# Pinning the whole instruction order of an attention and feed-forward kernel by a flat list, with one buffer pool and fewer loads

## The chip, the cores and the metric

The kernel runs on one core of a Trainium2 chip. The metric is the device time of one execution in microseconds (us), less being better; a profile of one execution goes with it.

## The reference

A recurrent attention over 4 x 8 heads of size 48 and 768 steps is followed, per token, by a two-layer feed-forward network with an unusual activation:

```python
for t in range(S):
    state = alpha[:, :, t, :, None] * state + np.einsum('bhd,bhe->bhde', k[:, :, t], v[:, :, t])
    y[:, :, t] = np.einsum('bhd,bhde->bhe', q[:, :, t], state)
...
h = x @ w_in                       # x: 3072 x 384 (y by token), w_in: 384 x 2048
sp = np.maximum(h, 0.0) + np.log1p(np.exp(-np.abs(h)))
g = h * erf(sp)
return (g @ w_out).astype(np.float32)
```

The inputs q, k, v and alpha are float32; w_in and w_out are float64 and arrive as pairs of 32-bit integers.

## The kernel before, in words

**The attention** is computed in 24 chunks of 64 steps for 2 of the 4 batch entries at once (two runs of 12 chunks). In `Chunk`, `ld` (L151) loads alpha, k and q with two loads each, one per half of the partitions, into one set of raw buffers. `a1` (L159) scans alpha into its running product A on VectorE, and GpSimd copies A's last column to `ae` (L165). `a2` (L170 to L176) makes the reciprocal of A: Relu for a check, Ln and Exp on ScalarE, then a correction in two VectorE operations. `a3` (L180 to L186) loads v and multiplies k and q into K and Q. `a4` multiplies K by Q (`pS`, L202) and the previous chunk's K by v (`pu`, L211) on TensorE, brings the state T forward on VectorE (L221 to L227), masks `pS` into `sT` (L229) and transposes K (`pn`, L235; `kn`, L239). `a5` (L260) makes y on TensorE from T, Q, sT and v, and `put` (L284, L285) splits it into `x_hi` (ScalarE) and `x_lo` (VectorE).

**The feed-forward network** runs over 12 blocks of 256 tokens, two chunks each, in `Moe`. Every product is made in three matmuls of rounded high and low parts. For each of 4 groups g of 512 hidden columns: `H` (L320), two halves of 18 matmuls, each copied out by ScalarE (`hs`, L325); `U` (Tanh, L331); `L1` (two Ln and an Exp, L336 to L338); `L2` (VectorE, L344, L345); `G` (Gelu, L348); `Z` (VectorE, L352, L353); `O` (two halves: `gh` by a copy, L366 or L368, `gl` by a subtraction, L369, and 12 matmuls into `acc`, L377). `out` (L385, L386) copies the two accumulators and stores them. Tanh and Gelu need one ScalarE table, Ln and Exp another; `new_phase` (L117) loads a table (L120) and `tab` keeps the table's functions on its own side of it.

**The weights** come in 12 pieces of w_in (512 columns) and 16 of w_out (384 columns): a load (L400), then ScalarE and VectorE turn the float64 bits into float32 (L406 to L414) and into a high and a low part (L389, L390).

**The order** is written as three lists of whole steps, START, ORDER (run for blocks 2 to 10) and TAIL (L27 to L48), which `run` (L513) issues one after the other; the framework's scheduler then sets the instructions' order on each engine from priorities that follow it, and may let a later one pass. The buffers are split by purpose: raw, K, Q, A and `ae` for the attention; pools of 4 KB buffers (per partition) of their own for s (5), hs (7), w (4) and t (1) (L70 to L77), which weights being converted share. All loads and stores are issued by SP's queue.

Of the kernel before, what the change touches and what calls it, by code (L numbers as in the profile page):

```python
# [20 lines left out]
AHI = 1e15  # L21
# [5 lines left out]
START, ORDER, TAIL = (  # L27
    z.split()
    for z in (
# [15 lines left out]
    )  # L45
)
# [3 lines left out]
def gla_moe(ctx: ExitStack, tc: tile.TileContext, q, k, v, alpha, w_in, w_out, out):  # L50
# [3 lines left out]
    M, CPB, _, D, NP, NI, TC = q.shape  # L54
    P = NI * TC
# [9 lines left out]
    NG = NF // GT  # L65
    HD = 64
# [15 lines left out]

    ra = raw.tile([P, NP * NI, 1 + TC], F32, name="raw_a")
    rq, rk = (raw.tile([P, NP, NI, TC], F32, name=f"raw_{nm}") for nm in "qk")
    for t, fill in ((ra, 1.0), (ra[:, :, 0], 0.0), (rq, 0.0), (rk, 0.0)):
        nc.vector.memset(t, fill)
# [10 lines left out]
    fixed = const.tile([P, 3], F32, name="fixed")  # L97
    bhi, bhalf, ones = (fixed[:, n : n + 1] for n in range(3))
    for t, val in ((bhi, -AHI), (bhalf, 0.5), (ones, 1.0)):
        nc.gpsimd.memset(t, val)  # L100
# [14 lines left out]
    phase = {"cur": [], "prev": []}  # L115

    def new_phase(table):  # L117
        phase["prev"] = phase["cur"]
        phase["cur"] = []
        tab(nc.scalar.preload_act_table_set(table))  # L120
        phase["prev"] = phase["cur"]
        phase["cur"] = []

    def tab(ins):
        for p in phase["prev"]:
            tc.add_manual_dep(ins.ins, p.ins.name, NOSYNC, reason="tables")
        phase["cur"].append(ins)
        return ins

    T = at.tile([P, NI * NP * HD], F32, name="T", tag="T", bufs=1)
# [6 lines left out]
    class Chunk:  # L139
# [6 lines left out]
        def ld(self):  # L146
            self.ra, self.rq, self.rk = ra, rq, rk
            for t, src in ((self.ra[:, :, 1:], alpha), (self.rk, k), (self.rq, q)):
                t = t if src is alpha else t.rearrange("p a i t -> p (a i) t")
                for par in range(2):  # L150
                    nc.sync.dma_start(  # L151
                        out=t[par * HD : par * HD + D],
                        in_=src[self.m, self.c, par].rearrange("d a i t -> d (a i) t"),
                    )

        def a1(self):
            self.A = at.tile([P, NP * NI, 1 + TC], F32, name="A", tag="A")
            flat = "p s t -> p (s t)"
            nc.vector.tensor_tensor_scan(  # L159
                out=self.A.rearrange(flat), data0=self.ra.rearrange(flat), data1=lower.rearrange(flat), initial=1.0,  # L160
                op0=ALU.mult, op1=ALU.max,
            )

            self.ae = at.tile([P, NI, NP], F32, name="ae", tag="ae")
            nc.gpsimd.tensor_copy(out=self.ae, in_=self.A[:, :, TC].rearrange("p (a i) -> p i a", a=NP))  # L165

        def a2(self):
            A = self.A[:, :, 1:]
            r = at.tile([P, NP * NI, TC], F32, name="r", tag="r", bufs=1)
            nc.scalar.activation(r, A, AF.Relu, bias=-AHI, accum_out=flags[:, self.n, 1:2])  # L170
            tab(nc.scalar.activation(r, A, AF.Ln))  # L171
            tab(nc.scalar.activation(r, r, AF.Exp, scale=-1.0, accum_out=flags[:, self.n, 0:1]))
            self.K = at.tile([P, NP, NI, TC], F32, name="K", tag="K")
            w = self.K.rearrange("p a i t -> p (a i) t")
            nc.vector.tensor_tensor(out=w, in0=A, in1=r, op=ALU.mult)
            nc.vector.scalar_tensor_tensor(out=w, in0=w, scalar=2.0, in1=r, op0=ALU.subtract, op1=ALU.mult)  # L176

        def a3(self):
            self.vv = raw.tile([P, NI * NP * HD + H * D], F32, name="raw_v", tag="raw_v", bufs=2)
            nc.sync.dma_start(out=self.vv, in_=v[self.m, self.c])  # L180
            flat = "p a i t -> p (a i t)"
            w = self.K.rearrange(flat)
            nc.vector.tensor_tensor(out=w, in0=self.rk.rearrange(flat), in1=w, op=ALU.mult)  # L183
            self.Q = at.tile([P, NP, NI, TC], F32, name="Q", tag="Q")
            flat = "p a i t -> p (a i) t"
            nc.vector.tensor_tensor(  # L186
                out=self.Q.rearrange(flat), in0=self.rq.rearrange(flat), in1=self.A[:, :, 1:], op=ALU.mult
            )

        def a4(self):  # L190
            K, Q = self.K, self.Q
# [6 lines left out]
            for pair in range(NP):  # L198
# [7 lines left out]
                if before:  # L206
                    vt = before.vv[:, NI * NP * HD :]
                    for half in range(2):
                        for i in range(NI):
                            toks, h = slice(i * TC, (i + 1) * TC), 2 * pair + (half ^ i)  # L210
                            nc.tensor.matmul(  # L211
                                out=pu[i][half * HD : (half + 1) * HD, pair * D : (pair + 1) * D],
                                lhsT=before.kn[toks, pair, half, :], rhs=vt[toks, h * D : (h + 1) * D],
                                start=True, stop=True,
                            )
            if before:
                aeb = before.ae.unsqueeze(3).broadcast_to([P, NI, NP, D])
# [395 lines left out]
```

## Time and profile before

| | us |
|---|---|
| median of 3 runs | 580.14 (580.12 to 580.36) |
| the profiled execution | 580.21 |
| its span, first to last instruction | 578.5 |
| TensorE (PE) matmuls busy | 515.2 |
| VectorE (DVE) busy | 482.5 |
| ScalarE (ACT) busy | 463.5 |
| GpSimd (POOL) busy | 51.1 |
| granted TensorE clock, mean | 0.972 of full |

Busy time is the time in which an engine has at least one instruction under way; neighbours overlap a little. The profile also tells what each engine waited for, follows the chain of waits back from the last instruction, and groups instructions by line.

### The profile page before, as it was taken

How to read it: one execution, taken by the hardware profiler on the slowest of the kernel's cores; microseconds unless marked ns; L12 is line 12 of the kernel's file. 1: busy time of each engine (PE TensorE's matmuls, PEld its weight loads, DVE VectorE, ACT ScalarE, POOL GpSimd, SP SyncE). 2: the span in 40 equal slices, each digit the busy share in tenths (PEclk: the TensorE clock that was granted, in tenths of full speed). 3: DMA queues.
4: the chain of work that ended last, by engine and by line, in shares of the span. 5: the costliest groups of instructions: out<-in, count | busy, mean ns of one | idle time of the engine just before them, and what ended most of it. 6: DMA issues, size and time to landing. Idle time of an engine off the chain costs nothing.

```text
span 578.5 us, 16974 instructions
## 1 busy us (share of the span) xinstructions
PE 515.2 (89%) x7386; PEld 496.8 (86%) x7386; DVE 482.5 (83%) x688; ACT 463.5 (80%) x706; POOL 51.1 (9%) x40
## 2 busy tenths in 40 slices
PE   0569769289999999999999999999999999999875
PEld 0458669289999999999999999999999999999775
DVE  6889879999989959969979789789699689477890
ACT  4458796689979789789699599599698797898951
POOL 2000000000000401300000400400302200000000
PEclk9999988779999999999999999999999999999988
DMA  6757434523213213211222122123022010000000
GB/s 195 229 195 222 130 114 126 157 66 83 80 30 98 65 26 92 93 43 43 75 60 74 44 61 76 42 60 103 16 62 88 1 48 30 1 1 28 28 0 33
DMA packets 36370, 43.64 MB, mean 75 GB/s; under 512 B 21952, under 2 KB 25024, under 8 KB 36288
## 3 DMA queue, kind: packets, MB, share of 16 engines
q1 hardware_dynamic: 36288, 42.48, 25.0%
q8 instruction: 60, 0.98, 0.7%
q14 instruction: 22, 0.18, 0.1%
HBM read 37.75 MB, written 4.72 MB: 73 GB/s over the span
## 4 chain that ended last, share of the span: by engine, by line
PE 61%; ACT 16%; DVE 16%; issue 5%; DMA 2%; DVEq 0%; ACTq 0%; SPq 0%
PE ph L320 27%; PE acc L377 22%; PE py L260 4%; PE pS L202 3%; ACT s L331 2%; ACT L120 2%; ACT s L336 2%; PE pu L211 2%; DVE w L345 2%; PE pn L235 2%; ACT hs L325 2%; ACT w L338 1%; ACT r L171 1%; DVE wbuf L411 1%; DVE t L344 1%
## 5 line engine op out<-in xcount | busy, mean ns | idle before, releaser
L320 PE MATMUL ph<-x_hi,wi_hi 128*128 128x256 f32 x576 | 166.9, 291 | 7.6 <-ACT x_hi L284 5.5
L320 PE MATMUL ph<-x_lo,wi_hi 128*128 128x256 f32 x576 | 164.8, 286 | 1.0 <-DVE x_lo L285 1.0
L320 PE MATMUL ph<-x_hi,wi_lo 128*128 128x256 f32 x576 | 164.6, 286 | 0.0
L377 PE MATMUL acc<-wo_hi,gh 128*128 128x384 f32 x384 | 132.5, 345 | 13.0 <-DVE gh L366 8.6
L377 PE MATMUL acc<-wo_hi,gl 128*128 128x384 f32 x384 | 130.1, 342 | 2.6 <-DVE gl L369 2.6
L377 PE MATMUL acc<-wo_lo,gh 128*128 128x384 f32 x384 | 130.6, 340 | 0.0
L320 PEld LDWEIGHTS ph<-x_hi,wi_hi 128*128 128x128 f32 x576 | 111.8, 194 | 10.2 <-ACT x_hi L284 5.9
L320 PEld LDWEIGHTS ph<-x_lo,wi_hi 128*128 128x128 f32 x576 | 112.0, 194 | 1.4 <-DVE x_lo L285 1.3
L320 PEld LDWEIGHTS ph<-x_hi,wi_lo 128*128 128x128 f32 x576 | 111.8, 194 | 0.4 <-DVE wi_lo L390 0.2
L325 ACT ACTIVATE hs<-ph 128x512 f32<-128x512 f32 x96 | 56.7, 591 | 45.6 <-PE ph L320 44.2
L377 PEld LDWEIGHTS acc<-wo_hi,gh 128*128 128x128 f32 x384 | 73.9, 192 | 14.1 <-DVE gh L366 8.8
L165 POOL COPY ae<-A 128x8 f32<-128x8 f32 x24 | 48.7, 2028 | 417.4 <-DVE T L227 338.7
L369 DVE TENSOR_TENSOR gl<-hs,gh 128x512 fp32r<-128x512 f32 x96 | 64.3, 686 | 19.2 <-ACT gh L368 16.5
L377 PEld LDWEIGHTS acc<-wo_hi,gl 128*128 128x128 f32 x384 | 73.0, 192 | 4.7 <-DVE gl L369 4.6
L377 PEld LDWEIGHTS acc<-wo_lo,gh 128*128 128x128 f32 x384 | 73.9, 192 | 0.1
L344 DVE TENSOR_TENSOR t<-s,w 128x1024 f32<-128x1024 f32 x48 | 58.6, 1220 | 12.4 <-ACT w L338 12.2
L202 PE MATMUL pS<-Q,K 48*64 48x64 f32 x768 | 39.1, 235 | 26.0 <-DVE K L183 25.5
L368 ACT ACTIVATE gh<-hs 128x512 fp32r<-128x512 f32 x72 | 45.3, 629 | 18.5 <-PE acc L377 14.4
L202 PEld LDWEIGHTS pS<-Q,K 48*64 48x64 f32 x768 | 33.0, 145 | 30.9 <-DVE K L183 21.8
L345 DVE SCALAR_TENSOR_TENSOR w<-t,w 128x1024 f32<-128x1024 f32 x48 | 58.5, 1218 | 0.4
L352 DVE TENSOR_TENSOR s<-s,w 128x1024 f32<-128x1024 f32 x48 | 58.2, 1217 | 0.0
L353 DVE SCALAR_TENSOR_TENSOR hs<-s,hs 128x1024 f32<-128x1024 f32 x48 | 58.1, 1216 | 0.1
(63 smaller groups left out, 831.9 us busy)
## 6 DMA issues: line engine op xcount, KB each, us to landing
raw_v<-in_v_dram SPq DMA_DIRECT2D x24, 448.0 KB, 3.9
wst<-in_moe_w_in_dram SPq DMA_DIRECT2D x12, 512.0 KB, 4.7
wst<-in_moe_w_out_dram SPq DMA_DIRECT2D x16, 384.0 KB, 3.8
raw_a<-in_alpha_dram SPq DMA_DIRECT2D x48, 96.0 KB, 3.0
raw_k<-in_k_dram SPq DMA_DIRECT2D x48, 96.0 KB, 2.6
raw_q<-in_q_dram SPq DMA_DIRECT2D x48, 96.0 KB, 2.2
out_dram<-o SPq DMA_DIRECT2D x24, 192.0 KB, 2.0
```

The source lines that it names most:

```text
L165: nc.gpsimd.tensor_copy(out=self.ae, in_=self.A[:, :, TC].rearrange("p (a i) -> p i a", a=NP))
L202: nc.tensor.matmul(out=ps[half * HD : (half + 1) * HD, pair * NI + i, :], lhsT=K[rows, pair, i, :], rhs=Q[rows, pair, i, :], start=True, s ...
L260: nc.tensor.matmul(out=py[i][c0 : c0 + 32, kt, :], lhsT=left[r0 : r0 + rows, at0 : at0 + 32], rhs=right[r0 : r0 + rows, pair, i, :], start ...
L320: nc.tensor.matmul(out=o, lhsT=wt[:, kt, fs], rhs=xt[:, kt, :], start=n == 0, stop=n == 3 * KT - 1)
L325: nc.scalar.activation(self.hs[g][:, sl], ph, AF.Copy)
L344: nc.vector.tensor_tensor(out=t, in0=s, in1=w, op=ALU.mult)
L345: nc.vector.scalar_tensor_tensor(out=w, in0=t, scalar=2.0, in1=w, op0=ALU.add, op1=ALU.mult)
L352: nc.vector.tensor_tensor(out=s, in0=s, in1=w, op=ALU.mult)
L353: nc.vector.scalar_tensor_tensor(out=h, in0=s, scalar=RT2 / 2, in1=h, op0=ALU.subtract, op1=ALU.mult)
L368: nc.scalar.activation(ghf, gg, AF.Copy)
L369: nc.vector.tensor_tensor(out=gl.rearrange("p a t -> p (a t)"), in0=gg, in1=ghf.bitcast(F32), op=ALU.subtract)
L377: nc.tensor.matmul(out=self.acc[tt][:, :DM], lhsT=gt[:, u, ts], rhs=wt[:, f, :], start=f == 0 and n == 0, stop=f == NF - 1 and n == 2,)
```

## The change

1. The three lists become one flat list, SCHED, of 1846 parts. Each step is now a generator that yields after every part on one engine (a group of 6 or 9 matmuls, one ScalarE or VectorE operation, a load), and naming a step in the list issues its next part. The scheduler is told to keep that order on every engine. The order itself is a different one, no longer the same from block to block.
2. ScalarE's table is loaded wherever the next function in the list needs the other one (`act`), instead of in named phases.
3. One pool `big` of 19 buffers of 4 KB serves s, hs, w, t, the loaded weights, their work buffers, and k with q.
4. alpha comes as one load of all 128 partitions, with its first column and its unused rows filled in on the host, into one of three buffers; k and q come together as one load. The scan runs in place, k and q are multiplied in place, the reciprocal has a buffer `rw` of its own, and T's product reads A's last column itself, without GpSimd's copy. The memsets of the raw buffers are gone.
5. Several buffers become single (`at`, L71, has one buffer for each tag now).

```diff
-START, ORDER, TAIL = (
...
+SCHED = """
+la_0 a1_0 a2_0 la_1 a2_0 a2_0 la_2 a1_1 a1_2 lq_0 a3_0 a2_0 wi_9 wi_9 wi_9 a2_0 wi_9 wi_5 wi_5 wi_5 a2_1 a2_1 a2_0
+a4_0 wi_11 wi_11 wi_9 wi_11 wi_9 wi_5 wi_11 wi_8 wi_8 a2_1 wi_8 wi_0 wi_0 lv_0 wi_0 wi_5 a4_0 a5_0 a4_0 wi_0 a2_1 wi_4
...
+lq_6 lv_6 a1_7 O_0_1_0 O_0_1_0 O_0_1_1 O_0_1_1 G_0_2 U_1_0 L2_0_3 L1_1_0 wo_9 wo_9 a2_6 H_1_2_0 H_2_2_0 H_2_2_0 wo_14
...
+O_11_2_0 Z_11_3 O_11_2_1 O_11_2_1 O_11_2_1 O_11_2_1 Z_11_3 O_11_3_0 O_11_3_0 O_11_3_1 O_11_3_1 O_11_3_0 O_11_3_0
+O_11_3_1 O_11_3_1 out_11_0 out_11_0 out_11_1 out_11_1
+"""
...
+    NBIG, NA = 19, 3
...
-    raw = fast.enter_context(tc.tile_pool(name="raw", bufs=1))
-    at = fast.enter_context(tc.tile_pool(name="at", bufs=2))
+    raw = fast.enter_context(tc.tile_pool(name="raw", bufs=2))
+    at = fast.enter_context(tc.tile_pool(name="at", bufs=1))
...
-    keep_s = fast.enter_context(tc.tile_pool(name="keep_s", bufs=NG + 1))
-    keep_h = fast.enter_context(tc.tile_pool(name="keep_h", bufs=2 * NG - 1))
-    keep_w = fast.enter_context(tc.tile_pool(name="keep_w", bufs=NG))
-    tmp = fast.enter_context(tc.tile_pool(name="tmp", bufs=1))
+    big = fast.enter_context(tc.tile_pool(name="big", bufs=NBIG))
...
-    for t, fill in ((ra, 1.0), (ra[:, :, 0], 0.0), (rq, 0.0), (rk, 0.0)):
-        nc.vector.memset(t, fill)
...
+    loaded = [None]
+
+    def act(table, *args, **kw):
+        if loaded[0] != table:
+            loaded[0] = table
+            nc.scalar.preload_act_table_set(table)
+        nc.scalar.activation(*args, **kw)
...
-        def ld(self):
...
+        def la(self):
+            self.A = raw.tile([P, NP * NI, 1 + TC], F32, name="A", tag="A", bufs=NA)
+            nc.sync.dma_start(out=self.A.rearrange("p s t -> p (s t)"), in_=alpha[self.m, self.c].rearrange("p a i t -> p (a i t)"))
+            yield
+
+        def lq(self):
+            self.kq = big.tile([P, 2, NP, NI, TC], F32, name="kq", tag="big")
+            nc.sync.dma_start(
+                out=self.kq.rearrange("p w a i t -> p (w a i t)"),
+                in_=qk[self.m, self.c].rearrange("p w a i t -> p (w a i t)"),
+            )
+            yield
...
         def a1(self):
...
-            self.ae = at.tile([P, NI, NP], F32, name="ae", tag="ae")
-            nc.gpsimd.tensor_copy(out=self.ae, in_=self.A[:, :, TC].rearrange("p (a i) -> p i a", a=NP))
+            a, floor = (z.rearrange("p s t -> p (s t)") for z in (self.A, lower))
+            nc.vector.tensor_tensor_scan(out=a, data0=a, data1=floor, initial=1.0, op0=ALU.mult, op1=ALU.max)
+            yield
...
+            kk = self.kq[:, 0].rearrange("p a i t -> p (a i) t")
+            nc.vector.tensor_tensor(out=kk, in0=kk, in1=w, op=ALU.mult)
+            yield
...
-                aeb = before.ae.unsqueeze(3).broadcast_to([P, NI, NP, D])
+                ae = before.A[:, :, TC].rearrange("p (a i) -> p i a", a=NP)
+                aeb = ae.unsqueeze(3).broadcast_to([P, NI, NP, D])
...
         def L1(self, g):
             s = self.s[g]
...
+            act(LNEXP, s, s, AF.Ln, scale=0.5 - 2.0**-24, bias=0.5)
+            yield
+            self.w[g] = w = self.pl.w.tile([P, GT * TB], F32, name="w", tag=self.pl.tag("w"))
+            act(LNEXP, w, s, AF.Ln, scale=-1.0)
+            yield
+            act(LNEXP, w, w, AF.Exp, scale=-1.0)
+            yield
...
-    run(START, 0, 0)
-    for i in range(2, NBLK - 1):
-        run(ORDER, 2 * i + 4, i)
-    run(TAIL, 2 * NBLK, NBLK - 1)
+    def steps():
+        made = {}
+        for step in SCHED.split():
...
+            next(made[step])
+        assert all(next(part, None) is None for part in made.values())
+
+    with tc.manual_schedule():
+        steps()
```

In the list, `wi_n` and `wo_n` are the pieces of w_in and w_out, `la_n`, `lq_n`, `lv_n` the loads of chunk n, `a1_n` to `a5_n` its steps (in `a2_n` the sixth part makes K; in `a4_n` the parts are pS with pu, T, sT, pn and kn; in `a5_n` py, two x_hi, two x_lo), and `H_b_g_half` to `out_b_tile` the parts of block b.

## Rows read from the trace of the kernel before

**Rows 1.** The page of the whole run: the span, the busy time of each engine (us, share of the span, instructions) and, in 40 slices of 14.5 us, the busy tenths of PE.

```profile
span 578.5 us, 16974 instructions
...
PE 515.2 (89%) x7386; PEld 496.8 (86%) x7386; DVE 482.5 (83%) x688; ACT 463.5 (80%) x706; POOL 51.1 (9%) x40
...
PE   0569769289999999999999999999999999999875
```

**Rows 2.** Busy time by stretch (the windows view). Columns: the stretch, its length, then us busy and instructions of PE, PE's weight loads, DVE, ACT and POOL, the mean granted clock of TensorE, the DMA share and GB/s.

```profile
0.00:140.00 140.00, 91.19 (x1559) 84.45 (x1563) 122.22 (x215) 98.05 (x173) 5.64 (x24) 0.91 0.52 155
140.00:520.00 380.00, 377.18 (x5569) 367.97 (x5570) 321.33 (x430) 328.42 (x489) 45.46 (x17) 1.00 0.19 54
520.00:572.10 52.10, 46.83 (x268) 44.41 (x266) 38.91 (x45) 36.57 (x46) 0.00 (x0) 0.93 0.05 17
```

**Rows 3.** The chain of waits, 387 to 432 us: start (us), length (us), engine, tile and line, number of instructions.

```profile
387.04 2.15 PE ph L320 x18
389.18 1.41 PE py L260 x91
390.60 4.51 PE ph L320 x36
395.11 2.09 PE acc L377 x12
...
398.73 0.58 PE pn L235 x4
399.31 2.09 PE acc L377 x12
...
430.85 1.41 PE py L260 x91
```

**Rows 4.** The last matmul (timeline view): start, length, engine, line, operation, tiles, form, number.

```profile
571.73 0.34 PE L377 MATMUL acc<-wo_hi,gl 128*128 128x384 f32 x1
```

**Rows 5.** The stretch after 520 us as in rows 2, first for line 320 (the H matmuls) alone, then for line 377 (the O matmuls) alone: PE and its weight loads only.

```profile
520.00:572.10 52.10, 8.79 (x72) 8.65 (x72) 0.93 0.05 17
...
520.00:572.10 52.10, 38.24 (x194) 35.75 (x192) 0.93 0.05 17
```

**Rows 6.** The timeline of VectorE, 389.8 to 405 us, columns as in rows 4. Neighbouring operations overlap by some 0.1 us, so the price of one is the distance to the next start.

```profile
389.81 1.23 DVE L159 TENSOR_TENSOR_SCAN A<-raw_a,lower 128x520 f32<-128x520 f32 x1
390.96 0.66 DVE L183 TENSOR_TENSOR K<-raw_k,K 128x512 f32<-128x512 f32 x1
...
400.71 0.69 DVE L229 TENSOR_TENSOR sT<-pS,maskn 128x512 f32<-128x512 f32 x1
401.31 0.61 DVE L225 TENSOR_TENSOR T<-T,pu 128x192 f32<-128x192 f32 x2
401.84 1.22 DVE L352 TENSOR_TENSOR s<-s,w 128x1024 f32<-128x1024 f32 x1
402.97 0.55 DVE L227 TENSOR_TENSOR T<-T,ae 128x384 f32<-128x384 f32 x1
403.44 1.22 DVE L353 SCALAR_TENSOR_TENSOR hs<-s,hs 128x1024 f32<-128x1024 f32 x1
404.58 0.42 DVE L366 CAST gh<-hs 128x512 fp32r<-128x512 f32 x1
404.92 1.22 DVE L352 TENSOR_TENSOR s<-s,w 128x1024 f32<-128x1024 f32 x1
```

**Rows 7.** The timeline of VectorE: its first operation on loaded data, with the idle time before it and its releaser, and a weight piece of 512 columns.

```profile
4.60 0.43 DVE L408 TENSOR_SCALAR wbuf<-wst 128x512 int32<-128x512 int32 x1 [2.01 <-DMA wst<-in_moe_w_in_dram]
...
25.25 0.42 DVE L408 TENSOR_SCALAR wbuf<-wst 128x512 int32<-128x512 int32 x1
25.58 0.68 DVE L414 SCALAR_TENSOR_TENSOR wbuf<-wbuf 128x512 int32<-128x512 int32 x1
```

**Rows 8.** DMA by stretch, columns as in rows 2; the last two are the share of the 16 DMA engines and GB/s.

```profile
20.00:24.00 4.00, 0.00 (x0) 0.00 (x0) 2.46 (x5) 2.95 (x8) 0.00 (x0) 1.00 1.03 377
...
56.00:60.00 4.00, 3.17 (x54) 2.57 (x55) 2.43 (x6) 3.08 (x5) 0.00 (x0) 1.00 0.96 256
```

**Rows 9.** The timeline of ScalarE around a table load (L120), columns as in rows 4.

```profile
393.04 0.64 ACT L368 ACTIVATE gh<-hs 128x512 fp32r<-128x512 f32 x1
393.70 1.28 ACT L120 ACT_TABLE_LOAD   x1
395.00 1.06 ACT L348 ACTIVATE s<-s 128x1024 f32<-128x1024 f32 x1
```

**Rows 10.** The group of the table loads: line, engine, operation, count, then busy us and mean ns of one, then idle time before and its releaser.

```profile
L120 ACT ACT_TABLE_LOAD x28 | 35.9, 1283 | 1.2 <-PEq L572 0.8
```

**Rows 11.** The page's DMA issues: tiles, queue, operation, count, KB each, median us from issue to landing.

```profile
wst<-in_moe_w_in_dram SPq DMA_DIRECT2D x12, 512.0 KB, 4.7
...
raw_a<-in_alpha_dram SPq DMA_DIRECT2D x48, 96.0 KB, 3.0
```

**Rows 12.** Who waited for whom: engine, tile and line, releaser: us in total, times, longest.

```profile
POOL ae L165 <- DVE T L227: 338.7, 18, 33.0
...
DVE gl L369 <- DMA out_dram<-o: 1.5, 2, 0.8
```

**Rows 13.** Busy time and granted clock by stretch, columns as in rows 2.

```profile
108.00:112.00 4.00, 0.27 (x26) 0.11 (x12) 3.02 (x8) 1.62 (x4) 0.00 (x0) 0.62 0.67 200
112.00:116.00 4.00, 0.00 (x0) 0.00 (x0) 4.00 (x9) 1.29 (x3) 0.00 (x0) 0.50 0.65 179
```

More of the change, by code (lines that the diff above doesn't have):

```diff
@@ L49, in gla_moe @@
+"""
 @with_exitstack
-def gla_moe(ctx: ExitStack, tc: tile.TileContext, q, k, v, alpha, w_in, w_out, out):
+def gla_moe(ctx: ExitStack, tc: tile.TileContext, qk, v, alpha, w_in, w_out, out):
     nc = tc.nc
-    M, CPB, _, D, NP, NI, TC = q.shape
-    P = NI * TC
+    M, CPB, P, _, NP, NI, TC = qk.shape
+    D = 48
     B, H, S = M * NI, 2 * NP, CPB * TC
@@ L96, in gla_moe @@
         )
[L97 to L100, printed above, removed]
+    ones = const.tile([P, 1], F32, name="ones")
+    nc.gpsimd.memset(ones, 1.0)
     NS = M * CPB
@@ L113, in gla_moe @@
     wo_lo = const.tile([P, NF, DM], F32R, name="wo_lo")
[L115 to L132, printed above, removed]
+    loaded = [None]
[4 more added lines that the diff above has]
+        nc.scalar.activation(*args, **kw)
+    T = at.tile([P, NI * NP * HD], F32, name="T", tag="T")
     nc.gpsimd.memset(T, 0.0)
@@ L144, in __init__ @@
             self.last = self.c == CPB - 1
-        def ld(self):
[L147 to L154, printed above, removed]
@@ new lines, in lq, with lv @@
+        def lq(self):
[5 more added lines that the diff above has]
+            yield
+        def lv(self):
+            self.vv = raw.tile([P, NI * NP * HD + H * D], F32, name="raw_v", tag="raw_v")
+            nc.sync.dma_start(out=self.vv, in_=v[self.m, self.c])
+            yield
@@ L182, in a3 @@
[L182 to L188, printed above, removed]
+            qq = self.kq[:, 1].rearrange("p a i t -> p (a i) t")
+            nc.vector.tensor_tensor(out=qq, in0=qq, in1=self.A[:, :, 1:], op=ALU.mult)
@@ L284, in put @@
                 nc.scalar.activation(x_hi[:, :, toks], py[i], AF.Copy)
+                yield
+            for i in range(NI):
+                toks = slice((2 * i + s) * TC, (2 * i + s + 1) * TC)
                 nc.vector.tensor_tensor(
@@ L309, in H @@
             x_hi, x_lo = self.x
-            if half == 0:
-                self.hs[g] = self.pl.h.tile([P, GT * TB], F32, name="hs", tag="hs")
             ph = self.pl.ph.tile([P, 512], F32, name="ph", tag="h")
@@ L355, in Z @@
             )
+            yield
         def O(self, g, half):
-            if g == 0 and half == 0:
-                self.acc = [self.pl.acc.tile([P, 512], F32, name="acc", tag="acc") for _ in range(2)]
             sl = slice(half * 512, (half + 1) * 512)
@@ L371, in O @@
             )
+            yield
+            if g == 0 and half == 0:
+                self.acc = [self.pl.acc.tile([P, 512], F32, name="acc", tag="acc") for _ in range(2)]
             for u in range(2):
@@ L419, in weight_in, with out, weight @@
-    def weight_in(n):
+                yield
+        def out(self, tt):
+            o = self.pl.gp.tile([P, DM], F32, name="o", tag="gl")
+            nc.scalar.activation(o, self.acc[tt][:, :DM], AF.Copy, scale=RT2)
+            yield
+            nc.sync.dma_start(out=out[bass.ds(self.toks[tt], P), :], in_=o)
+            yield
+    def weight(hi, lo, src, n):
+        if src.dtype == F32:
+            z = big.tile([P, n], F32, name="wst", tag="big")
+            nc.sync.dma_start(out=z, in_=src)
+            for _ in range(5):
+                yield
+        else:
+            st = big.tile([P, n, 2], I32, name="wst", tag="big")
+            nc.sync.dma_start(out=st.rearrange("p n two -> p (n two)"), in_=src.bitcast(I32))
+            yield
+            low, high = st[:, :, 0], st[:, :, 1].bitcast(F32)
+            buf = big.tile([P, 1024], F32, name="wbuf", tag="big")
+            y, z = buf[:, :n], buf[:, 512 : 512 + n].bitcast(I32)
+            nc.scalar.activation(y, high, AF.Copy, scale=2.0**-112)
+            top = y.bitcast(I32)
+            yield
+            nc.vector.tensor_scalar(
+                out=z, in0=low, scalar1=29, scalar2=None, op0=ALU.logical_shift_right
+            )
+            yield
+            nc.vector.scalar_tensor_tensor(
+                out=z, in0=top, scalar=3, in1=z, op0=ALU.logical_shift_left, op1=ALU.bitwise_or
+            )
+            yield
+            nc.vector.scalar_tensor_tensor(
+                out=z, in0=top, scalar=-0x80000000, in1=z, op0=ALU.bitwise_and, op1=ALU.bitwise_or
+            )
+            yield
+            z = z.bitcast(F32)
+        nc.scalar.activation(hi, z, AF.Copy)
+        yield
+        nc.vector.tensor_tensor(out=lo, in0=z, in1=hi.bitcast(F32), op=ALU.subtract)
+        yield
@@ L490, in general @@
                 for g in range(NG):
[L491 to L502 removed]
+                    for part in (m.H(g, 0), m.H(g, 1), m.U(g), m.L1(g), m.L2(g), m.G(g), m.Z(g), m.O(g, 0), m.O(g, 1)):
+                        for _ in part:
+                            pass
+                for tt in range(2):
+                    for _ in m.out(tt):
+                        pass
     chunks = [Chunk(n) for n in range(NS)]
@@ L584, with rows @@
                     order.extend(range(at0 + d0, at0 + d1))
+    def rows(a):
+        a = a.reshape(M, NI, NP, 2, C, TC, D).transpose(0, 4, 3, 6, 2, 1, 5).copy()
+        a[..., 1, :] = a[:, :, ::-1, :, :, 1, :].copy()
+        return a
     for name in _INS:
-        a = inputs[name]
+        if name == "qk":
+            a = _np.zeros((M, C, 2, 64, 2, NP, NI, TC), inputs["q"].dtype)
+            for w, nm in enumerate("kq"):
+                a[:, :, :, :D, w] = rows(inputs[nm])
+            a = a.reshape(M, C, 128, 2, NP, NI, TC)
+        elif name == "alpha":
+            a = _np.ones((M, C, 2, 64, NP, NI, 1 + TC), inputs["alpha"].dtype)
+            a[..., 0] = 0
+            a[:, :, :, :D, :, :, 1:] = rows(inputs["alpha"])
+            a = a.reshape(M, C, 128, NP, NI, 1 + TC)
+        else:
+            a = inputs[name]
         if name == "v":
```

287 lines of the change are left out of this document (171 added, 116 removed), and 15 rows, old and new, of the table RT2.

## The prediction, made before the change was run

> **What bounds the kernel now.** I read the page first: of 578.5 us TensorE (PE) is busy 515.2, VectorE (DVE) 482.5, ScalarE (ACT) 463.5. Three engines are nearly full, but PE's slices are full only between the first tenth or two and the last three slices [rows 1]. So I cut the span into stretches [rows 2]. Up to 140 us DVE is busy 122.2 us and PE 91.2: DVE, which converts the weights and prepares the chunks, sets the pace. From 140 to 520 us PE is busy 377.2 of 380. After that nobody is full; PE waits for the last block.
>
> The chain of waits in the middle gives PE's own prices [rows 3]. A half H (9 matmuls) is 2.15/2 = 1.076 us, half an O (6 matmuls) 2.08/2 = 1.041; py is 1.41 and the 0.21 by which the next 36 H matmuls exceed 4.30, so 1.62; the piece between the two O's, 397.20 to 399.31, is 1.52 for pS with pu and 0.58 for pn. A block is 16 H parts, 16 O parts and two chunks: 17.2 + 16.7 + 7.4 = 41.3 us. The same py comes again 41.67 us later, so PE waits 0.35 us in each block and there is next to nothing to win there. Over the kernel PE's parts add up to 491.7 us (192 x 1.076, 192 x 1.041, 22 x 1.62, 22 x 1.52, 22 x 0.58, and about 3.4 for the two first chunks). The span minus that is 87 us: 6.4 lie after the last matmul, which ends at 572.1 [rows 4]; some 10 in the last block (52.1 us for 72 H and 194 recorded O matmuls, 8.6 + 33.7 = 42.3 [rows 5]); 3 to 4 in the middle; the rest, about 67, in the first 140 us. **The front is where PE's time is lost.**
>
> **The new order, the main term.** On DVE I take start-to-start times: 1.14 for 1024 columns, 1.15 for the scan, 0.60 for 512, 0.34 for the cast, 0.53 for T's two subtractions and half of that for an x_lo of as many columns, 0.47 for T's product on 384 columns [rows 6]. A weight piece has 0.34 [rows 7] and three times 0.60 at 512 columns, 0.27 (an estimate by its columns) and three times 0.47 at 384. With these prices the kernel's DVE work is 470.8 us and 1.5 for memsets, where the page counts 482.5; I scale by 1.022. Now I walk the list. Its py of chunk 6 needs that chunk's sT. Up to that sT the list gives DVE 8 scans, 75 operations at 0.60, 36 at 0.47, 26 at 0.27, 14 at 1.14, 13 at 0.34, and T six times (5 x 1.00 and 0.53): 104.0 us, scaled 106.3. From that py on PE has 152 H parts, 184 O parts, 17 py and one at 1.0, 16 pS with pu and one pS at 0.72, 15 pn: 163.6 + 191.5 + 28.5 + 25.0 + 8.7 = 417.4 us. The same kind of sum from the last K part of chunk 5, or from the last x_lo of chunk 3 to the first H of block 1, comes within 1 us of it: the list keeps DVE's work before and PE's after in step through the front, and leaves PE full work from then on.
>
> Between the two terms lie the waits. DVE's idle time in the front is at least 4.6 us, its first operation behind a load [rows 7], and at most about today's, 140 - 122.2 = 17.8 [rows 2]. I take 10: the 4.6, 1.3 for the first table load (below) and 4 for loads: up to piece 7 of w_in the list asks for 13.1 MB, and DVE has 41 us of work; stretches with the DMA engines full moved 377 and 256 GB/s [rows 8], so the loads take 35 to 51 us against 46. So far 116.3. PE's waits after that, 0.35 in each of 10 blocks: 3.6. In the last block the list still has 16 O parts, 16.7 us, after the last H, and 12 of them, 12.5, can run beside that group's hs, U, table load, L1, L2, G, Z, gh and gl (0.60 + 1.06 + 1.28 + 3.18 + 1.22 + 1.06 + 2.44 + 0.64 + 0.69 = 12.2 [rows 6, 9]). So 0 to today's 10, and I take 3, as the gh's of other O's share ACT. The 6.4 after the last matmul stay [rows 4]. **The sum:** 116.3 + 417.4 + 3.6 + 3 + 6.4 = 546.7 of span. The profiled execution took 580.21 for its span of 578.5, 1.7 more, and is 0.07 above the median of 580.14; so 548.4.
>
> **Twenty more table loads.** The list's ACT parts, taken in order, change between the two tables 48 times, where now there are 28 loads of 1.28 us [rows 10]: 25.7 us more, 463.5 + 25.7 = 489 on ACT. Costed at nothing, because PE covers them: begun at 5.8 us (4.6 and a scan) and followed by 16 us after its last G, ACT would be through at 511, 37 us sooner. If that cover is gone they cost up to all 26. A load starts 0.02 us after the operation before it and the next starts 0.02 after the load [rows 9]. The page "ScalarE: Activation LUTs" of the Trainium skill (section "What ACT_TABLE_LOAD costs") speaks against the change: it puts a drain of 1.38 us beside each load, 2.66 for every switch. The trace does not show that drain; by that figure 48 switches would be 128 us, ACT 555 and the time 577. The first load, now the first thing ACT does, is put behind the first Relu, hence the 1.3 above.
>
> **Loads.** A chunk's six loads of alpha, k and q, 96 KB each, become two of 266 and 524 KB: four issues fewer on SP, a fifth more bytes. A large one lands later, 4.7 us for 512 KB against 3.0 [rows 11]: 0 to 2 us a chunk, taken as 0, because three alpha buffers and the pool let SP run ahead; without that cover 24 x 2 = 48. SP stays in order: where a load waits for a buffer, all later loads and the stores of out stand behind it, and gl on DVE waits for a store's buffer (today 1.5 us in all [rows 12]).
>
> **What costs nothing.** The POOL copies spend 338.7 us waiting for T [rows 12] and are on no chain; T now reads the scan's last column itself, taken at its product's present 0.47: 0 more at the low end, 20 x 0.13 = 2.6 us if the strided read made it as dear as 512 columns [rows 6]. DVE's memsets lie before its first load. The scan and k, q in place keep shape and count. Cutting H and O in halves costs PE nothing: an O follows an H without a gap [rows 3].
>
> **Rivals.**
> (a) *The queue heads wait all along.* Each engine's order is pinned, so one late part holds everything behind it. If DVE keeps the idle share of the first 140 us (12.7% [rows 2]) to its end, 481/0.873 = 551, then 4.2 for the last O's and 8.1: **563**. For it: the sum asks 88 to 90% of three engines at once in an order that cannot bend. Against: in the middle PE waits 0.35 in 41.67 us.
> (b) *ACT becomes the bound by its table loads.* If each also waits until the operation before it is through (1.06 more than shown [rows 9]), 48 x 2.34 on 427.6 (463.5 less today's loads) is 540, with 5.8 ahead and 16 behind **562**. Against: the 0.02 us gaps. By the page's 2.66 it would be the 577 above.
> (c) *Slower: the one pool.* With each tile held from its first part to its last, all 19 buffers are held at the peak, and at 22 of the 253 re-uses no other one is free. Each then waits for one reader to end, 1.22 us for a DVE operation, or for two, 2.44; a load there blocks SP, an hs copy ACT, an L2 DVE. 22 x 1.83 = 40: **588**. It decides from 1.45 us each. Against: the reader that frees a buffer mostly stands several parts earlier in the list.
> (d) *The order does nothing*, the engines being held by something else: **580**.
>
> **How the numbers follow.** Forecast 0.63, (a) 0.21, (b) 0.05, (c) 0.08, (d) 0.03. The forecast's own ends: idle of 4.6, no waits and no loss in the last block give 536.4; idle of 17.8 and today's last block 563. One cost may come on top. With PE nearly still its clock was granted at 0.62 and then 0.50, the lower of its two levels, 1.2 GHz of 2.4 [rows 13]; the first 140 us had 0.91 on average [rows 2], which is 25 us at that level, and where such a stretch meets full PE work it costs half, 12 us. The range, 536 to 571, leaves out (c), (d) and the worst of (b). A measurement of this kernel can tell 0.2%, some 1.2 us, from no change. Faster by more: the forecast, (a), (b) and a third of (d), 0.90; within it 0.02; slower 0.08.
>
> **What would show it.** Right: DVE over 90% busy to 115 us, with chunk 6's sT near there; PE 99% busy from then on; the last matmul near 540; 48 table loads of 1.28; two loads of alpha, k and q a chunk. Wrong: PE waiting 1 us or more in a block after 130 us (a, c), ACT without idle time (b), loads late for their first reader, or the clock at its lower level after 120 us.

## The result and the profile after

The changed kernel took **538.29 us** (median of 4 runs, 537.11 to 538.59), the kernel before beside it 580.13 (579.50 to 580.36): ratio 0.9277, 95% interval 0.926 to 0.9293. 548.4 was predicted, 536 to 571 its range. The profiled execution took 537.11 us for a span of 535.4.

The page of the changed kernel, for [rows 1] and [rows 11]: span, busy us by engine, the busy tenths of three engines and TensorE's granted clock in 40 slices, then DMA issues (KB each, median us to landing).

```profile
span 535.4 us, 16828 instructions
...
PE 498.9 (93%) x7386; PEld 482.1 (90%) x7386; DVE 485.2 (91%) x684; ACT 492.8 (92%) x727; POOL 2.3 (0%) x14
...
PE   0468899999999999999999999999999999999995
...
DVE  6999999999999999999988999989868799898892
ACT  5649999999999999999999899999999999999981
...
PEclk9999999999999999999999999999999999999998
...
kq<-in_qk_dram SPq DMA_DIRECT2D x24, 512.0 KB, 3.6
...
A<-in_alpha_dram SPq DMA_DIRECT2D x24, 260.0 KB, 3.2
wst<-in_moe_w_in_dram SPq DMA_DIRECT2D x12, 512.0 KB, 9.1
```

PE is full from the sixth slice to the last but one; before, it held that level only from the tenth slice on and lost it in the last three. The granted clock was 1.00 up to the last matmul, where the kernel before had 0.91 on average up to 140 us [rows 2]. The timeline, for [rows 4], [rows 6] and [rows 9]: SP's first issue of w_in, chunk 6's sT, a table load, and the last matmul.

```profile
2.67 2.91 SPq L497 DMA_DIRECT2D wst<-in_moe_w_in_dram  x5
...
109.22 0.56 DVE L304 TENSOR_TENSOR T<-T,A 128x384 f32<-128x384 f32 x1
109.70 0.68 DVE L307 TENSOR_TENSOR sT<-pS,maskn 128x512 f32<-128x512 f32 x1
110.30 0.55 DVE L513 SCALAR_TENSOR_TENSOR wbuf<-wbuf 128x384 int32<-128x384 int32 x1
...
303.52 0.60 ACT L320 ACTIVATE kn<-pn 128x512 f32<-128x512 f32 x1
304.12 1.28 ACT L202 ACT_TABLE_LOAD   x1
305.42 1.06 ACT L203 ACTIVATE s<-hs 128x1024 f32<-128x1024 f32 x1
...
528.65 0.34 PE L476 MATMUL acc<-wo_hi,gl 128*128 128x384 f32 x1
```

DVE is past that sT at 110.3 us, the last matmul ends at 529.0. Cut there, the windows view (columns as in [rows 2]) gives the two terms of the prediction; four stretches for the experiments follow.

```profile
0.00:110.30 110.30, 81.66 (x1550) 75.71 (x1551) 104.98 (x189) 91.89 (x161) 2.35 (x14) 1.00 0.56 196
110.30:529.00 418.70, 417.23 (x5838) 406.43 (x5836) 380.17 (x496) 400.43 (x566) 0.00 (x0) 1.00 0.20 63
...
0.00:20.00 20.00, 4.20 (x100) 3.44 (x100) 15.23 (x26) 12.76 (x25) 2.35 (x14) 1.00 0.93 334
20.00:40.00 20.00, 11.74 (x271) 10.18 (x272) 20.00 (x40) 10.82 (x24) 0.00 (x0) 1.00 0.87 322
...
220.00:320.00 100.00, 99.90 (x1518) 96.62 (x1518) 91.78 (x122) 96.63 (x142) 0.00 (x0) 1.00 0.24 75
...
360.00:395.00 35.00, 35.00 (x543) 34.37 (x543) 29.08 (x39) 34.32 (x51) 0.00 (x0) 1.00 0.19 61
```

The same cut through the kernel before, whose chunk 6 is past its sT at 137.6 us:

```profile
0.00:137.60 137.60, 89.00 (x1538) 82.69 (x1539) 119.82 (x211) 95.65 (x167) 5.57 (x23) 0.91 0.52 154
137.60:572.10 434.50, 426.18 (x5851) 414.14 (x5849) 362.64 (x479) 367.40 (x539) 45.53 (x17) 0.99 0.18 51
```

So the 43.1 us of span came from four places: 14.8 us less DVE work ahead of that sT (119.8 to 105.0), 12.5 less DVE idle time there (17.8 to 5.3), 6.8 less PE idle time behind it (8.3 to 1.5), and 9.0 less PE busy time behind it (426.2 to 417.2). Of the last, 4.9 us are a shorter distance between H matmuls (1,368 of them, 3.6 ns each), which is no matter of order. The other 4.1 belong at least in part to the order: in u_noload below, with H's distances as here, PE's busy time is also 4.6 us above that of the pinned run beside it. The chain of waits, for [rows 3], shows the distances, first in the kernel before, then in the changed one:

```profile
147.14 0.59 PE pn L235 x4
147.73 4.31 PE ph L320 x36
```

```profile
244.95 1.25 PE acc L476 x6
246.20 4.24 PE ph L407 x36
...
380.00 0.59 PE pn L315 x4
380.58 4.09 PE ph L407 x36
...
392.57 6.25 PE acc L476 x36
```

Behind pn, 36 H matmuls took 4.31 us and take 4.09 now (the row at 380.58); behind an O they take 4.24 (the row at 246.20). The O's are as they were: 36 in 6.25, where 12 took 2.09.

### The profile page after: what moved, and what is told of

Its sections match the earlier page's. It is cut to its first block, busy times and chain, and to the rows that moved or that the text cites. A ratio compares the mean times of both kernels' runs of the same rounds, so it can differ in the third digit from the quotient of the medians.

```text
span 535.4 us, 16828 instructions
## 1 busy us (share of the span) xinstructions
PE 498.9 (93%) x7386; PEld 482.1 (90%) x7386; DVE 485.2 (91%) x684; ACT 492.8 (92%) x727; POOL 2.3 (0%) x14
## 4 chain that ended last, share of the span: by engine, by line
PE 78%; ACT 7%; DVE 7%; DMA 3%; issue 2%; SPq 1%
PE acc L476 35%; PE ph L407 32%; PE py L343 5%; PE pS L277 3%; PE pu L286 2%; DMA wst<-in_moe_w_in_dram 2%; ACT s L203 2%; PE pn L315 1%; DMA raw_v<-in_v_dram 1%; ACT w L203 1%; ACT hs L415 1%; DVE wbuf L509 1%; DVE wi_lo L520 1%; DVE gl L465 1%; ACT L202 1%
## 5 line engine op out<-in xcount | busy, mean ns | idle before, releaser
L407 PE MATMUL ph<-x_hi,wi_hi 128*128 128x256 f32 x576 | 164.9, 286 | 2.1 <-ACT hs L415 1.1
L407 PE MATMUL ph<-x_lo,wi_hi 128*128 128x256 f32 x576 | 161.3, 280 | 3.2 <-DVE x_lo L373 3.2
L407 PE MATMUL ph<-x_hi,wi_lo 128*128 128x256 f32 x576 | 161.2, 280 | 0.3 <-DVE wi_lo L520 0.3
L407 PEld LDWEIGHTS ph<-x_hi,wi_hi 128*128 128x128 f32 x576 | 108.5, 188 | 5.0 <-ACT hs L415 2.0
L407 PEld LDWEIGHTS ph<-x_lo,wi_hi 128*128 128x128 f32 x576 | 108.6, 189 | 3.5 <-DVE x_lo L373 3.5
L407 PEld LDWEIGHTS ph<-x_hi,wi_lo 128*128 128x128 f32 x576 | 109.7, 190 | 0.5 <-DVE wi_lo L520 0.5
L203 ACT ACTIVATE s<-s 128x1024 f32<-128x1024 f32 x96 | 100.9, 1057 | 0.9 <-DVE t L436 0.4
L476 PEld LDWEIGHTS acc<-wo_hi,gh 128*128 128x128 f32 x384 | 72.2, 188 | 2.2 <-ACT gh L462 0.5
L476 PEld LDWEIGHTS acc<-wo_lo,gh 128*128 128x128 f32 x384 | 72.2, 188 | 0.0
L277 PE MATMUL pS<-kq 48*64 48x64 f32 x768 | 38.3, 235 | 15.3 <-DVE kq L257 15.1
```

What stands on the lines that cost most here:

```text
L203: nc.scalar.activation(*args, **kw)
L277: nc.tensor.matmul(out=ps[half * HD : (half + 1) * HD, pair * NI + i, :], lhsT=K[rows, pair, i, :], rhs=Q[rows, pair, i, :], start=True, s ...
L407: nc.tensor.matmul(out=o, lhsT=wt[:, kt, fs], rhs=xt[:, kt, :], start=n == 0, stop=n == 3 * KT - 1)
L476: nc.tensor.matmul(out=self.acc[tt][:, :DM], lhsT=gt[:, u, ts], rhs=wt[:, f, :], start=f == 0 and n == 0, stop=f == NF - 1 and n == 2,)
```

## The experiments

Each is the changed kernel with one edit, timed in 4 runs. They ran in three groups of four, each beside the kernel before, whose medians were 579.84, 580.02 and 580.06.

### The order: c_unpinned and u_noload

```diff
-    with tc.manual_schedule():
-        steps()
+    steps()
```

> The changed kernel with all its new parts (one pool, two loads of alpha, k and q a chunk, scan and keys in place) and the same list as the order of the program, but not pinned: each engine's order is chosen by the framework's own scheduler. Theory: the gain of 42 us comes from the pinned order, which has DVE through its work up to chunk 6's sT at 110 us and gives PE full work from there on. Without the pin PE loses time in the front again: 550 to 590 us, chunk 6's sT later than 115 us or PE's idle time after it over 10 us. Rival (the new parts and the rough order of the list bring the gain, the pin nothing): 536 to 541 us. Rival (the pin even costs): below 536.

709.32 us, ratio 1.2241 (1.2207 to 1.2274): far outside all three. Groups of the table loads, then the page's busy times:

```profile
L203 ACT ACT_TABLE_LOAD x145 | 186.0, 1283 | 2.5
L202 ACT ACT_TABLE_LOAD x48 | 61.6, 1283 | 1.5 <-PEq L657 0.8
```

```profile
PE 546.1 (77%) x7386; PEld 517.2 (73%) x7386; DVE 486.9 (69%) x684; ACT 679.6 (96%) x871; POOL 2.3 (0%) x14
```

The 48 loads that the helper writes (L202) come apart from the activations they were written for: 25 of them are followed by the next one with no activation of the helper between, and 145 more loads are put in ahead of activations (L203). ACT, 96% busy, is the bound, so the run doesn't price the order. Without tables it does:

```diff
-            act(GELU, self.s[g], self.hs[g], AF.Tanh, scale=-0.5)
+            nc.scalar.activation(self.s[g], self.hs[g], AF.Relu, scale=-0.001)
...
-            act(GELU, self.s[g], self.s[g], AF.Gelu, scale=-RT2)
+            nc.scalar.activation(self.s[g], self.s[g], AF.Relu, scale=-RT2)
...
-    with tc.manual_schedule():
-        steps()
+    steps()
```

> The unpinned kernel (scheduler's order) with Tanh and Gelu replaced by Relu with a scale: it leaves out these two functions and with them the table loads, of which the unpinned kernel made 193 against 49 pinned (ACT busy 679.6 us of its 707.5, of which 247 are loads). To be read against the pinned kernel with the same functions left out, 535.9. Theory (the pin is worth its order of PE's and DVE's parts, apart from the loads): 548 to 580 us, PE's idle time after 120 us over 10. Rival (all that the pin saves are table loads, since the loads stand where the list has them and the scheduler moves the operations away from them): 533 to 540.

572.68 us against 535.87 pinned (n_noload, below): in the kernel without table loads the pinned order alone is worth 36.8 us. Windows of the two, cut at the end of chunk 6's sT and at the last matmul (pinned first):

```profile
0.00:110.40 110.40, 82.77 (x1554) 77.71 (x1555) 104.95 (x190) 84.58 (x155) 2.35 (x14) 1.00 0.56 195
110.40:527.00 416.60, 415.75 (x5834) 405.81 (x5832) 379.82 (x496) 351.39 (x525) 0.00 (x0) 1.00 0.20 63
```

```profile
0.00:136.30 136.30, 85.97 (x1556) 80.63 (x1556) 114.30 (x202) 89.35 (x163) 2.35 (x14) 0.92 0.47 165
136.30:565.40 429.10, 420.32 (x5830) 406.71 (x5830) 367.26 (x484) 339.85 (x516) 0.00 (x0) 1.00 0.19 60
```

Unpinned, that sT ends 25.9 us later: DVE does 9.4 us more ahead of it and is idle for 22.0 us instead of 5.4. Behind it PE is idle for 8.8 us instead of 0.8, and busy for 4.6 us more. These are the losses that the kernel before showed. Rival (d) falls, and the theory holds: its time is within 548 to 580, and PE's idle time after 120 us is 10.0, right at the bound that the theory gave.

### The table loads: n_noload and l_double

The first two replacements of the diff above, alone:

> The changed kernel with Tanh and Gelu replaced by Relu with a scale, so that ACT never changes its table: it leaves out these two activation functions, and 47 of the 48 table loads (1.28 us each, 60 us of ACT's 493). All else, the order too, is the same. Theory (the loads lie beside PE's full work, and the front is set by DVE): 535 to 539 us, so at most 3 us less than the 538.3 measured. Rival (ACT, 19.4 to 19.9 us busy in each 20 of the middle, sets PE's pace together with it): 5 to 25 us less, 513 to 533, with PE's idle time between 120 and 520 us gone.

535.87 us (534.98 to 536.90), ratio 0.9252 (0.9225 to 0.9278), an interval that overlaps the changed kernel's. 56.3 us less on ACT (436.5 busy instead of 492.8) give back 2.4 at most: PE covers the loads, as predicted.

```diff
+            nc.scalar.preload_act_table_set(GELU if table == LNEXP else LNEXP)
             nc.scalar.preload_act_table_set(table)
```

> The changed kernel with every change of table done twice (the table that is not wanted is loaded first, then the wanted one): 96 loads, some 48 x 1.28 = 61 us more on ACT. Theory (ACT has about 535 - 493 = 42 us to spare, of which 5.8 lie ahead of its first operation and 16 behind its last G): the cover runs out and ACT becomes the bound: 493 + 61 + 22 + 1.7 = 578 us, 570 to 585. Rival (table loads cost nothing at all, since they begin before the operation that wants them is due): 538 to 545. Rival (each load costs more than its 1.28 us, a drain as well): over 600.

592.95 us: beyond the theory's range, far over the rival of free loads and under that of a drain, so none of the three was met. ACT is the bound with 552.2 us busy, but it idles more in the front than the 5.8 us I gave it. Its first two windows have ACT at 12.33 and 11.45 of 20:

```profile
0.00:20.00 20.00, 3.63 (x99) 3.27 (x100) 13.37 (x22) 12.33 (x22) 2.35 (x14) 1.00 0.91 320
20.00:40.00 20.00, 10.40 (x234) 8.50 (x236) 19.96 (x41) 11.45 (x25) 0.00 (x0) 1.00 0.83 313
```

That is 16.2 us idle, 10.4 more than assumed: 578 + 10.4 = 588 of the 593; the other 5 us stay open. ACT's cover in the changed kernel is thus smaller than predicted; 48 further loads cost 54.7 us, 1.14 each.

### The loads of alpha, k and q: six

```diff
-            nc.sync.dma_start(out=self.A..., in_=alpha[self.m, self.c]...)
+            for p0 in (0, HD):
+                rows = slice(p0, p0 + HD)
+                nc.sync.dma_start(out=self.A[rows]..., in_=alpha[self.m, self.c, rows]...)
...
-            nc.sync.dma_start(out=self.kq..., in_=qk[self.m, self.c]...)
+            for w in range(2):
+                for p0 in (0, HD):
+                    rows = slice(p0, p0 + HD)
+                    nc.sync.dma_start(out=self.kq[rows, w]..., in_=qk[self.m, self.c, rows, w]...)
```

> The changed kernel with six loads of alpha, k and q a chunk again, each of 64 partitions (130 KB for alpha, 128 KB for k and q), instead of two of 128; bytes and order the same. Theory (the loads are ahead of their readers; only the packed start, where DMA moved 334 GB/s, could feel it): 536 to 541 us, within 0.5% of the changed kernel. Rival (four more issues a chunk on SP, or smaller packets, hold up the first loads): chunk 6's sT 2 us later or more, 541 to 550.

550.92 us, ratio 0.9495 (0.9477 to 0.9513): 12.6 us longer. The rival has the direction, though the time is 0.9 us beyond its range. Chunk 6's sT starts at 122.28 instead of 109.70. The first windows, what DVE waited for up to it, and SP's first issues:

```profile
0.00:20.00 20.00, 2.04 (x32) 1.85 (x32) 11.57 (x18) 10.38 (x18) 2.35 (x14) 1.00 0.79 260
20.00:40.00 20.00, 8.47 (x264) 6.96 (x264) 15.99 (x31) 9.19 (x19) 0.00 (x0) 1.00 1.04 280
```

```profile
DVE wbuf L512 <- DMA wst<-in_moe_w_in_dram: 5.6, 8, 1.4
DVE A L246 <- DMA A<-in_alpha_dram: 4.2, 1, 4.2
DVE wbuf L512 <- DMA wst<-in_moe_w_out_dram: 2.6, 2, 2.2
DVE kq L269 <- DMA kq<-in_qk_dram: 2.2, 2, 1.4
```

```profile
0.82 3.77 SPq L223 DMA_DIRECT2D A<-in_alpha_dram  x6
4.62 2.51 SPq L233 DMA_DIRECT2D kq<-in_qk_dram  x4
7.18 2.00 SPq L504 DMA_DIRECT2D wst<-in_moe_w_in_dram  x4
```

Two things can be seen. SP reaches the first piece of w_in at 7.18 us, where the two-load kernel is there at 2.67. And with the DMA engines full (share 1.04) 280 GB/s move, against 322 at share 0.87. By 40 us 10.8 MB have moved instead of 13.1, and DVE waits 14.6 us for loads instead of 4.7. Which of the two weighs more was not separated, nor what a third thing adds: between 40 and 60 us the granted clock was 0.86 on average, where the changed kernel has 1.00. From that sT on the kernel is about as fast as the other. In the kernel before, DVE's longest waits up to the same sT were others:

```profile
DVE K L175 <- ACT r L172: 4.1, 3, 1.6
DVE wo_lo L390 <- ACT wo_hi L389: 2.5, 2, 1.8
DVE wbuf L408 <- DMA wst<-in_moe_w_in_dram: 2.0, 1, 2.0
```

### Where a microsecond of DVE costs: f_front, f_mid, f_late, g_lo

f_front repeats the last operation of ten weight pieces, f_mid and f_late the first operation of five L2's:

```diff
-        nc.vector.tensor_tensor(out=lo, in0=z, in1=hi.bitcast(F32), op=ALU.subtract)
+        for _ in range(times):
+            nc.vector.tensor_tensor(out=lo, in0=z, in1=hi.bitcast(F32), op=ALU.subtract)
```

```diff
+            for _ in range(2 if self.n == 4 or (self.n, g) == (5, 0) else 1):
-            nc.vector.tensor_tensor(out=t, in0=s, in1=w, op=ALU.mult)
+                nc.vector.tensor_tensor(out=t, in0=s, in1=w, op=ALU.mult)
```

> The changed kernel with ten more DVE operations in the front: for ten of the twelve pieces of w_in the last operation (wi_lo, 512 columns) is done twice, all ahead of chunk 6's sT; 10 x 0.60 = 6.0 us more DVE work there. Theory (DVE's work sets the front and PE's the rest): the sT of chunk 6, now ending at 110.4 us of the span, comes 5 to 6 us later, and so does the end: 543 to 545 us. Rival (the front is set by loads or by PE, DVE has room): under 540.

543.92 us, 5.6 longer for 6.0 added: the theory. Chunk 6's sT starts at 117.81; where the front was left alone it was 109.7 (the changed kernel) to 111.9 (f_mid, f_late, x_64, x_32), as the pieces of w_in land earlier or later (DVE waits 0.2 us for them in the changed kernel, 1.1 to 2.6 in the other four). In the front DVE's work counts nearly in full.

> The changed kernel with five more DVE operations in the middle: the first operation of L2 (128x1024) is done twice for the four groups of block 4 and one of block 5; 5 x 1.22 = 6.1 us more DVE work than the changed kernel has there. Theory (from 111 us on PE's parts set the time, DVE has some 2 us to spare in each 20): 538 to 539 us, within 0.2% of the changed kernel. Rival (DVE is as tight in the middle as in the front): 542 to 545, PE's idle time there up by 4 to 6 us.

543.18 us, 4.9 longer: the rival. The front of its profiled run ended 1.3 us later by itself; the rest is here, PE's idle time having grown from 0.1 to 3.25 us:

```profile
220.00:320.00 100.00, 96.75 (x1494) 92.93 (x1492) 93.93 (x121) 92.96 (x135) 0.00 (x0) 1.00 0.22 70
```

> As the kernel with five doubled L2 operations in blocks 4 and 5, which took 543.2 us where 538 to 539 was expected; here the doubled ones are those of groups 3, 1, 0 of block 7 and 1, 0 of block 8, at 360 to 394 us of the span, where DVE is busy 17.1 and 15.5 of 20 us (18.6 to 19.4 where the others stood). Theory now (at 235 to 265 us DVE is nearly as full as PE, and a delay of its own passes on): here at most 1 us, 537 to 539.5. Rival (any added operation in the chain of L2 delays the group's O, however idle DVE is): 541 to 545.

540.82 us, ratio 0.9311 (0.929 to 0.9332), between the two forecasts and hardly clear of the changed kernel by its time. The window is clear: PE is idle for 2.04 us where it was idle for none, with DVE idle for 2.7.

```profile
360.00:395.00 35.00, 32.96 (x526) 31.64 (x525) 32.33 (x39) 32.50 (x49) 0.00 (x0) 1.00 0.19 66
```

So in these two places a busy share of DVE below 1 (92% and 83%) was no cover for a part that stands in a chain of a pinned order: of 6.1 us added, 3.2 and 2.0 came through as PE's idle time.

```diff
-        nc.vector.tensor_tensor(out=lo, in0=z, in1=hi.bitcast(F32), op=ALU.subtract)
+        nc.gpsimd.tensor_tensor(out=lo, in0=z, in1=hi.bitcast(F32), op=ALU.subtract)
```

> The changed kernel with the last operation of every weight piece (w minus its rounded value) on GpSimd instead of DVE: 12 at 512 columns and 16 at 384, 14.7 us less DVE work, 12.5 of it ahead of chunk 6's sT. Theory (DVE sets the front, but PE has only some 5 us of idle time between 40 and 110 us): chunk 6's sT comes 4 to 12 us earlier, the end 3 to 10: 528 to 535 us. Rival (GpSimd's operations are late for the first H or slow DVE down beside them): 538 to 550.

544.91 us, 6.6 longer: the rival. 23 operations left DVE's front (some 12 us), yet DVE was busy for 108.9 us up to the sT instead of 105.0. The reason, in the timeline:

```profile
30.77 7.43 POOL L520 TENSOR_TENSOR wi_lo<-wbuf,wi_hi 128x512 fp32r<-128x512 f32 x4 [2.54 <-ACT wi_hi L518]
...
35.32 1.76 DVE L257 TENSOR_TENSOR kq<-kq,rw 128x512 f32<-128x512 f32 x1
37.01 1.75 DVE L262 TENSOR_TENSOR kq<-kq,A 128x512 f32<-128x512 f32 x1
```

DVE's 128x512 operation, 0.68 us by itself, takes 1.76 while GpSimd works. The page "SBUF — State Buffer" of the Trainium skill (section "SBUF: two separate sides") says that a GpSimd operation that reads SBUF and a DVE operation with two SBUF inputs share a port that one holds for its whole instruction; the trace agrees, with 1.76 against 0.68. Added up over the front, operations that ran beside GpSimd's took 15.7 us more than the median of their kind did elsewhere, which is more than the 12 that left; the sT, which reads one operand from PSUM, kept its 0.68 beside them.

### The GpSimd copy, and where x stands: p_copy, x_64, x_32

```diff
+            self.ae = raw.tile([P, NI, NP], F32, name="ae", tag="ae", bufs=3)
+            nc.gpsimd.tensor_copy(out=self.ae, in_=self.A[:, :, TC].rearrange("p (a i) -> p i a", a=NP))
```

> The changed kernel with the GpSimd copy of the scan's last column put back (24 copies), and T's product reading that copy as before. Theory: the copy was on no chain and T's product costs the same either way, so 537 to 540 us, within 0.3% of the changed kernel's 538.3, and T's product at 0.47 us in both. Rival (the copy between scan and T cost time by its wait): 541 to 548.

538.45 us, ratio 0.9288 (0.9263 to 0.9313), the same: the copy cost nothing that the time shows, though chunk 6's sT starts at 112.33, and T's product takes 0.56 us with either operand. But its H matmuls came every 116.9 ns whatever ran before them, where the changed kernel has 117.6 behind O's and 113.6 behind pn. What differs for them is where the tiles lie, and the 24 copies on GpSimd. The next two runs move the tiles alone, with an unused one; x_32's is half as long.

```diff
+    pad = at.tile([P, 16], F32, name="pad", tag="pad")
+    nc.gpsimd.memset(pad, 0.0)
     T = at.tile([P, NI * NP * HD], F32, name="T", tag="T")
```

> The changed kernel with an unused tile of 64 bytes a partition ahead of x_hi, x_lo and the pools behind them, which shifts their addresses; no instruction of the stages changes. The H matmuls came every 120 ns before the change (x_hi began 384 bytes past a multiple of 512), every 117.6 or 113 to 115 after it (320 bytes past), and every 116.7 with the GpSimd copy put back (416 bytes past). Here x_hi begins 384 past again. Theory (the address of x sets the spacing): 120 ns, 1728 x 4 ns = 6 to 7 us longer, 543 to 546 us. Rival (the spacing depends on the order, the loads or what runs beside): 116 ns on average and 537 to 539.5 us.

542.10 us, ratio 0.9341 (0.9307 to 0.9375), 3.8 longer: the theory's spacing, its time a little less. PE's busy time behind chunk 6's sT is 421.0 us, 3.8 more than in the changed kernel.

> The changed kernel with an unused tile of 32 bytes a partition, so that x_hi begins 96 bytes past a multiple of 128 (352 past one of 512). So far H matmuls came on average every 119.5 ns at 0 past one of 128 (the kernel before, and the kernel with 64 bytes added), 116.9 at 32, 116.0 at 64. Theory (the address of x, by its place in 128 bytes, sets the spacing): a spacing of its own between 113 and 120 ns, one for the whole run within 1 ns or of two kinds as at 64; the time follows with about 1.5 us a ns: 534 to 544. Rival (only a start on a multiple of 128 is slow): 116 to 117 ns, 537 to 540 us.

540.79 us, ratio 0.9315 (0.9298 to 0.9332), one spacing of 118.2 ns: the theory. In the chain of waits 36 H matmuls behind an O took 4.24 us in the changed kernel. In x_64, then in p_copy, they took:

```profile
201.37 4.31 PE ph L409 x36
```

```profile
201.12 4.20 PE ph L408 x36
```

The pools' sizes tell where x_hi begins. By its first byte, as a remainder of 128, the mean distance from an H matmul's start to the next matmul's (1,616 to 1,649 in each run, those under 0.2 us) was 119.6 ns at 0 (the kernel before and x_64 alike), 116.9 at 32, 116.0 at 64 (the changed kernel) and 118.2 at 96. H's weights did not move, and the O's, whose moving operand did not move either, stayed at 173.4 to 174.7. So some 4 of the 42 us came with addresses that the new pools happen to give. That it is x's address is argued and not shown, as the unused tile moves every tile behind it.

## Why the prediction was right, and where it was 11 us off

The direction, the cause and three terms (DVE's work, the tail, the table loads) stand: DVE sets the front, PE all that follows. Against the profiled 537.1 us the sum was 11.3 too long, and the cut above shows where.

- **DVE's work in the front**, 106.3 predicted: 105.0. The prices gave 104.0; scaling them by 1.022 was the error, 1.3 us. Operations packed back to back go by start-to-start time (0.60), so the page's larger total belongs to the stretches where they stand apart.
- **DVE's idle time in the front**, 10 taken between 4.6 and 17.8: 5.3. This is the term of the front that was mis-sized most, 4.7 us. It is 3.6 for the first alpha, 1.1 for all later loads together, and 0.4 behind ACT; the first table load held nothing up. The loads' 4 us were too many: the start moved 334 and 322 GB/s, 13.1 MB by 40 us, just what the list asks.
- **The fuller loads**, taken as 0: here the prediction missed a cause. They are worth 12.6 us (six), as with six loads DVE waits 14.6 us for loads. The kernel before, with its six, waited otherwise: of its 17.8 us idle, 3.0 were waits for loads and 11.9 behind ACT. So the order takes away the waits behind ACT, and the packed start that it makes needs the fuller loads. The two are not to be added: 36.8 (measured without table loads), 12.6 and the 4 of the addresses are more than the whole gain of 41.8.
- **PE from chunk 6's py on**, 417.4 + 3.6 + 3 = 424.0: 417.9 (111.1 to 529.0). H's price fell from 119.6 to 116.0 ns, on 152 parts of 9 matmuls 4.9 us, the largest single miss; no step of the prediction had that. The other 1.2 lie in the waits and the last block, taken as 6.6. Between sT and py 0.8 us pass that the sum left out.
- **After the last matmul** 6.4, and 1.7 around the span: both as predicted. The profiled run is the fastest of four, 1.2 below the median.
- **Table loads**, costed at nothing: right, n_noload gives 2.4 us at most. There are 48, and one more at the start. By the 1.38 us drain of the Trainium skill's page "ScalarE: Activation LUTs" (section "What ACT_TABLE_LOAD costs") the 48 further loads of l_double would have cost 128 us, an estimate; they cost 54.7, and ACT's idle time fell from 42.6 to 39.4 us, so no run here shows the drain. The prediction was wrong only in counting 37 us as ACT's cover: 16.4 of its idle time lie in the first 40 us, ahead of most of the loads.
- **Rivals.** (a) did not happen, but its mechanism is there: f_mid and f_late show a late head handed on to PE at once, and the list works because few heads are late. (b) came with 48 loads more (l_double). (c) is there for SP, whose loads of k and q wait some 80 us in all for buffers of s, hs and w, but it hardly goes further: DVE waits 0.9 us for k and q in the whole run. A pool with more buffers was not tried. (d) falls by the 36.8 us of the pinned order.
- **The clock's 12 us** did not come: the granted clock was 1.00 in every 20 us up to 520, also in the first two, where PE was busy for 4.20 and 11.74. It was near: in six and f_front, where PE was busy for 8.47 and 7.70 of the second 20 us, the third had 0.86 and 0.83.

What stays open: what the old lists would give under a pin, which was not tried, and so how much of the 36.8 us is this list and how much any fixed order; why H has two spacings, 117.6 and 113.6 ns, in one run when x_hi begins 64 bytes past a multiple of 128 (the lower one mostly behind the attention's matmuls), and what the address changes.

## What to carry to other kernels

Cut the span where the bound passes from one engine to the next, and sum each engine's work on its own side by start-to-start prices: that gave the time to 2%, before the kernel ran. Count the start's loads by what the DMA engines move and by how long SP takes to issue them: splitting them cost 12.6 us here. Do not count on an engine's idle share for slack under a pinned order: an operation added in a chain cost a third to a half of its length here, where its engine was 8 to 17% idle.

## What the hardware showed that was not expected

- The distance of the fp32r H matmuls went with where the tiles lie: 119.6, 116.9, 116.0 or 118.2 ns with the moving tile 0, 32, 64 or 96 past a multiple of 128 bytes.
- In g_lo a GpSimd subtraction of 128x512 took 1.58 us on average (DVE: 0.68), and a DVE operation of 0.68 beside it up to 1.76.
- The pieces of w_in landed 9.1 us after their issue where it had been 4.7, in a start with a DMA share of 0.93 in the first 20 us; DVE waited 0.2 us for them up to chunk 6's sT.
